# Eight V tiles with copied key windows, one multiply for both table factors, and another order of work

## The chip, the core and the metric

The kernel runs on one core of a Trainium2 chip. A core has TensorE (PE, matrix multiply), VectorE (DVE), ScalarE (ACT), GpSimd (POOL) and SyncE (SP), which only issues transfers here, and 16 DMA engines that all queues share. TensorE reads SBUF and writes PSUM; VectorE and ScalarE take results out of PSUM. The metric is the device time of one execution in microseconds; the profile calls the stretch from the first to the last instruction the span.

## What is computed

Two independent layers on 2048 tokens of 448 features, bfloat16, their outputs side by side in one array of 2048 x 896.

- A is an attention with 16 heads of 28 features. A query at position s sees the keys at s, s-2, ..., s-14, eight of them. `qkv = x @ wqkv`; softmax of the eight scaled scores; weighted sum of the eight V rows; then `@ wo`.
- B is a diagonal state space layer: `h[t] = Lam_bar * h[t-1] + B_bar x[t]` with 448 complex states, and `y = 2 Re(C h) + x * Dskip`.

## The kernel before

**Layout.** Even and odd tokens never meet in A, since the dilation is 2. The kernel views 2048 tokens as 1024 pairs: `xA` holds the transposed input, 7 chunks of 128 features by 1024 pair positions, and every A tile carries both parities. A and B are interleaved in one program.

**A.** Projections contract 448 features per parity on half the rows of the array each: `pair` (lines 521 to 533) issues seven pairs of matmuls (lines 528 and 529), four in a first part and three in a second, with a GpSimd tick between. `V` is projected in nine blocks of 128 pair positions that start every 112 (`k0(b) = 112 * b`), so that each attention block has all its keys, its own and the 14 earlier ones, in one V tile: `Vt[:, par, b]`, with a column of ones behind each head's 28 features for the sum of weights. Blocks overlap in 16 positions, which are computed twice. Q and K are projected in three column ranges (256, 256 and 512 wide; in the text "wide" tiles are the last) by four feature groups. Attention block b then has two score nodes `s0b`, `s1b` (mask matmul L702, score matmuls L706), four exps (L712, `x..`), the weighted sum `a{b}` (32 matmuls, L724), a normalization `n{b}` on VectorE (L730, L731) and a DMA transpose `ot{b}` on SP (L736). Eight `w` tiles multiply by `wo`.

**B.** Four state groups k and two halves hf of time: `b{hf}{k}` (L764) projects the input, `be` evacuates it, VectorE rotates by a cosine/sine table (`ma`, then `ri`), scans (`sc`, L798), rotates back (`mb`, then `ro`) into `h`, and `y`/`z` tiles (L962 to L976) make the output. `ma` and `mb` are the function `mul`: for the three full groups one multiply of a 2 x 512 tile by the cosine row (L777) and one by the sine row (L778); for the small group two of 512 (L780, L781). The tables come from ScalarE: `t2` (L448) and `t4` (L454); only after them does it load the exp table. B's output matrices `C1`, `C2` and the skip product `Gm` (`g0`, `g1`) are built on the way.

**Order.** `Plan` (lines 33 to 113) lists nodes with a cost per engine, what they depend on, which ring of buffers they take from and which they free. It plays them engine by engine on its own clock and always starts the ready node with the lowest rank; `RANK` (line 27) gives each family of nodes an offset and a slope, and nodes that free PSUM go first. A node that can run on ScalarE or VectorE goes to the one that comes free first. The result is a fixed order for each queue. PSUM is a ring "mm" of four two-bank buffers. SP's queue is one list: input transposes, weight loads, then WT transposes, CT transposes, the OT transposes and the stores, each waiting at the head for its own data.

In that order the scores `s00` stand on TensorE behind V, the narrow Q/K tiles and one wide tile (q032); the other seven wide tiles lie between the first attention blocks and B's first projections.

Of the kernel before, what the change touches and what calls it, by code (L numbers as in the profile page):

```python
# [7 lines left out]
BF16 = mybir.dt.bfloat16  # L8
# [8 lines left out]
NB = 9  # L17
# [6 lines left out]
SCALE = float(DH) ** -0.5  # L24


RANK = {"v": (-247.7, 33.131), "q0": (-32.25, 20.848), "q1": (-1351, 261.899), "s": (-328.09, 66.43), "a": (312.95, 100.698), "b0": (348.52, -7.748),
        "b1": (2537.88, -155.645), "d0": (308.87, 213.856), "d1": (1776.4, -98.058), "l": (1991.99, 151.071), "t": (810.76, -33.643), "tk": (305.69, 160.366),
        "xd": (2014.82, -97.299), "cg": (910.27, 8.203), "ch": (1106.04, 1.621), "g": (869.44, 168.173), "y": (701.29, 136.506), "w": (1120.33, 1.167),
        "gu": (1198.03, -204.258), "q2": (787.17, -9.125), "wp": (320.49, 73.04)}  # L30


class Plan:
# [183 lines left out]
def kernel(  # L217
# [40 lines left out]
    tmpB = t_([128, 3584], F32, "tmpB", "rB")  # L258
    Kt = t_([128, 4, 2, NP], BF16, "Kt")
    Qt = t_([128, 4, 2, NP], BF16, "Qt")  # L260
    Vt = t_([128, 2, NB, H, 29], BF16, "Vt")
    Pb = [t_([128, 4, 4, 128], BF16, f"P{i}") for i in range(3)]
    msk = t_([128, 2, 128], BF16, "msk")
    mst = t_([32, 4, 128], BF16, "mst", "rG")
# [39 lines left out]
    SP.dma_start(natW[64:128, 3, D:2 * D], B_B_im[384:448, :])  # L304
    SP.dma_start(Pt[0:64, :], B_B_im[384:448, :])
    SP.dma_start(Pt[64:128, :], B_B_re[384:448, :])
    xbar_x(xB, xB2, 0, 256)
    xbar_x(xB, xB2, 256, 512)


    def sel(o, i, pat, op, fill, base, ch):
# [29 lines left out]
    gms += [lambda e, g=g: G.tensor_copy(msk[32 * g:32 * g + 32, :, :], msk[0:32, :, :]) for g in range(1, 4)]  # L341

    def g_one(e, a):
        G.memset(Vt[:, a, :, :, 28:29].rearrange("p b h o -> p (b h) o"), 1.0)

    def g_zero(e, i):
        if i < 3:
# [190 lines left out]
        behind(k, h["done"][1])  # L538


    plan = Plan({"mm": 4, "P": 3, "O": 3, "wt": 2, "u": 3, "rv": 1, "rs": 1, "ab": 1})
    lazy = {}

    def node(name, cost, fn, deps, rank, **kw):
# [94 lines left out]
    def k0(b):  # L639
        return 112 * b  # L640
# [7 lines left out]
    def at_x(t):  # L648
        return (5.8, 7.3, 9.4, 10.2, 12.0, 12.8, 13.7, 14.6)[(t - 1) // 128]
    vn = {}  # L650
    for b in range(NB):
        h = {}

        def pe(part, b=b, h=h):
            if part == 0:
                h["ps"] = unit()
            pair(h, part, h["ps"], D, lambda o, k: xA[o:o + 64, k, k0(b):k0(b) + 128], lambda o, k: Wv[o:o + 64, k, :])

        def ev(e, b=b, h=h):
            evac(e, Vt[:, :, b, :, 0:28], h["ps"][:, :, 0:D].rearrange("p a (h d) -> p a h d", h=H))  # L660
        n0, n1 = halves(f"v{b}", 0.188, pe, [vw], ("v", b), h, at_x(k0(b) + 128))
        vn[b] = node(f"ev{b}", ab(2 * D), ev, [n1], ("v", b), frees=[(n0, 0)])
    qn = {}
    CH = ((0, 256), (256, 512), (512, 1024))
    for c, (t0_, t1_) in enumerate(CH):
# [21 lines left out]
    for b in range(NB):  # L687
        n = nq(b)
        hb_ = [{}, {}]
        cs = [c for c, (lo, hi) in enumerate(CH) if lo < max(q0(b) + n, k0(b) + 128) and hi > min(q0(b), k0(b))]  # L690
        dep = [qn[q, s, c] for q in range(2) for s in range(4) for c in cs]
        xs = []
        for par in range(2):
            h = hb_[par]
            r = ("s", 2 * b + par)

            def pe(e, par=par, b=b, n=n, h=h):
                c0 = 0 if b == 0 else 16
                u = h["s"] = [unit(), unit()]
                at = lambda g: u[g // 2][:, g % 2]  # L700
                for g in range(4):
                    PE.matmul(at(g)[:, 0:4 * n].rearrange("p (s q) -> p s q", s=4), msk[32 * g:32 * g + 32, 0, :],  # L702
                              msk[32 * g:32 * g + 32, 1:2, c0:c0 + n].to_broadcast((32, 4, n)), start=True, stop=False, skip_group_check=True)
                for s in range(4):
                    for g in range(4):
                        PE.matmul(at(g)[:, s * n:s * n + n], Kt[32 * g:32 * g + DH, s, par, k0(b):k0(b) + 128],  # L706
                                  Qt[32 * g:32 * g + DH, s, par, q0(b):q0(b) + n], start=False, stop=(s == 3), skip_group_check=True)
            i = 2 * b + par

            def ex(e, z, i=i, n=n, h=h):  # L710
                P = h["P"] = Pb[i % 3]
                ACT.activation(P[:].rearrange("p s g q -> p g s q")[:, 2 * z:2 * z + 2, :, 0:n],  # L712
                               h["s"][z][:, :, 0:4 * n].rearrange("p g (s q) -> p g s q", s=4), ACTF.Exp, scale=SCALE)
            n1 = node(f"s{par}{b}", {"P": 0.45}, pe, dep + gm, r, alloc="mm", n=2, mode="q")
            x1 = node(f"x{par}{b}0", {"A": 0.00090 * 8 * n + 0.01}, lambda e, ex=ex: ex(e, 0), [n1, t4], r, alloc="P", frees=[(n1, 0)])
            x2 = node(f"x{par}{b}1", {"A": 0.00090 * 8 * n + 0.01}, lambda e, ex=ex: ex(e, 1), [x1], r, frees=[(n1, 1)])
            xs += [x1, x2]
        h = {}

        def pv(e, b=b, h=h, hb_=hb_):  # L720
            av = h["av"] = unit()
            for par in range(2):
                for hd in range(H):
                    PE.matmul(av[:, par, 29 * hd:29 * hd + 29], hb_[par]["P"][:, hd // 4, hd % 4, :], Vt[:, par, b, hd, :], start=True, stop=True)  # L724

        def nm(e, b=b, n=n, h=h):
            O = h["O"] = wk.tile([128, 2 * D], BF16, tag="O", name="O", bufs=3)
            rc = rcs[0:n, b, :, :]
            avv = h["av"][:, :, 0:29 * H].rearrange("p a (h c) -> p a h c", c=29)
            V.reciprocal(rc, avv[0:n, :, :, 28])  # L730
            V.tensor_tensor(O[0:n, :].rearrange("p (a h d) -> p a h d", a=2, h=H), avv[0:n, :, :, 0:DH],  # L731
                            rc.unsqueeze(3).to_broadcast((n, 2, H, DH)), ALU.mult)
        n3 = node(f"a{b}", {"P": 0.93}, pv, xs + [vn[b]] + g_1 + g_z, ("a", b), alloc="mm", frees=[(xs[0], 0), (xs[2], 0)])
        n4 = node(f"n{b}", {"V": 1.42}, nm, [n3, g_r], ("a", b), alloc="O", frees=[(n3, 0)])
        avs.append(n4)
        ot[b] = node(f"ot{b}", {"S": 1.25}, lambda e, b=b, n=n, h=h: SP.dma_start_transpose(OT()[:, :, q0(b):q0(b) + n], h["O"][0:n, :]),  # L736
                     [n4, t4], b, frees=[(n4, 0)], lat=2.1)
# [16 lines left out]
    for hf in range(2):  # L754
        for k in range(4):
# [13 lines left out]
                evac(e, u[:, 0:n, :], h["ps"][:, 0:n, :])  # L769

            def mul(e, src, k=k, h=h, big=big):
                c, s = tab[:, 0, k, :], tab[:, 1, k, :]
                a = h["a"] = wk.tile([128, 2, HALF], BF16, tag="ra", name="ra", bufs=1)
                x = h[src]
                if big:
                    b = h["b"] = wk.tile([128, 2, HALF], BF16, tag="rb", name="rb", bufs=1)
                    V.tensor_tensor(a[:], x[:], c.unsqueeze(1).to_broadcast((128, 2, HALF)), ALU.mult)  # L777
                    V.tensor_tensor(b[:], x[:], s.unsqueeze(1).to_broadcast((128, 2, HALF)), ALU.mult)  # L778
                else:
                    V.tensor_tensor(a[:, 0], x[:, 0], c, ALU.mult)  # L780
                    V.tensor_tensor(a[:, 1], x[:, 0], s, ALU.mult)  # L781

            def ri(e, k=k, h=h, big=big):
                a = h["a"]
                v = h["v"] = wk.tile([128, 2, HALF], BF16, tag="rv", name="rv", bufs=1)
                if big:
                    b = h["b"]
                    V.tensor_tensor(v[:, 0], a[:, 0], b[:, 1], ALU.add)
                    V.tensor_tensor(v[:, 1], a[:, 1], b[:, 0], ALU.subtract)
                else:  # L790
                    V.tensor_tensor(v[0:64, 0], a[0:64, 0], a[64:128, 1], ALU.add)
                    V.tensor_tensor(v[64:128, 0], a[64:128, 0], a[0:64, 1], ALU.subtract)

            def sc(e, i, k=k, hf=hf, h=h):
                if i == 0:
# [5 lines left out]
            def ro(e, k=k, hf=hf, h=h, big=big):  # L801
                hb, a = hbuf(hf), h["a"]
                to = slice(1, HALF + 1)
                if big:
                    b = h["b"]
                    V.tensor_tensor(hb[:, k, to], a[:, 0], b[:, 1], ALU.subtract)
                    V.tensor_tensor(hb[:, k + 4, to], a[:, 1], b[:, 0], ALU.add)
                    if hf == 0:
                        V.tensor_copy(ini[:, k:k + 5:4], hb[:, k:k + 5:4, HALF])
                else:  # L810
                    V.tensor_tensor(hb[0:64, 3, to], a[0:64, 0], a[64:128, 1], ALU.subtract)
                    V.tensor_tensor(hb[64:128, 3, to], a[64:128, 0], a[0:64, 1], ALU.add)
                    if hf == 0:
                        V.tensor_copy(ini[:, 3:4], hb[:, 3, HALF:HALF + 1])
            rb_, rd_ = (f"b{hf}", k), lambda off, hf=hf, k=k: (f"d{hf}", k, off)
            n1 = node(f"b{hf}{k}", {"P": 3.03 if big else 1.52}, pe, ([wtx[k], wtx[k + 4]] if big else [wtx[k]]) + ([xb1] if hf else []),
                      rb_, alloc="mm", at=24.8)
            n2 = node(f"be{hf}{k}", ab(1024 if big else 512), ev, [n1], rb_, alloc="u", frees=[(n1, 0)])
            m1_ = node(f"ma{hf}{k}", {"V": 1.25 if big else 0.8}, lambda e, mul=mul: mul(e, "u"), [n2, t4], rd_(0), alloc="ab", frees=[(n2, 0)])
            x = ri_ = node(f"ri{hf}{k}", {"V": 0.75 if big else 0.86}, ri, [m1_], rd_(-0.1), alloc="rv", frees=[(m1_, 0)])  # L820
            for i in range(2 if big else 1):
                x = node(f"sc{hf}{k}{i}", {"V": 1.18}, lambda e, i=i, sc=sc: sc(e, i), [x] + ([rout[0, k]] if hf else []), rd_(-0.2),
                         alloc="rs" if i == 0 else None, frees=[(ri_, 0)] if i == (1 if big else 0) else [])
                if i == 0:
                    s0 = x
            m2_ = node(f"mb{hf}{k}", {"V": 1.25 if big else 0.8}, lambda e, mul=mul: mul(e, "s"), [x, t4], rd_(-0.3), alloc="ab", frees=[(s0, 0)])
            free_ = list(wp.values()) if hf == 0 else qdone + vdone + [rout[0, j] for j in range(4)]
            rout[hf, k] = node(f"ro{hf}{k}", {"V": 0.9}, ro, [m2_] + free_, rd_(-0.4), frees=[(m2_, 0)])

# [218 lines left out]
```

## Time and profile before

| What | us |
|---|---|
| median of 14 runs (137.22 to 140.28) | 137.97 |
| profiled execution | 137.74 |
| its span | 136.0 |
| TensorE busy, share of the span | 127.4, 94% |
| VectorE busy | 109.6, 81% |
| ScalarE busy | 89.7, 66% |
| first exp starts | 38.68 |
| last matmul ends | 131.98 |

In the profile, L528 is line 528 of the kernel. A group line gives engine, operation, what it writes and reads, how often, the busy time, the mean ns of one, and the idle time before it with what ended it. A step is the time from one start to the next on an engine; since the end of one instruction overlaps the start of the next, it is shorter than the duration shown. PSUM casts on ScalarE have a step of 0.80 for 896 columns and 0.47 for 512, on VectorE 1.0 and 0.6.

### The profile page before, as it was taken

The numbers are of one execution on the slowest core, as the hardware profiler recorded it, in microseconds if no ns is written. First come the engines' busy times: TensorE is split into PE (matmuls) and PEld (weight loads), VectorE is DVE, ScalarE is ACT, GpSimd is POOL, SyncE is SP. The second block draws the span as 40 slices with busy tenths as digits, with TensorE's granted clock in tenths as the row PEclk, the third lists the DMA queues.
The fourth block names the chain that finished last, engine by engine and source line by source line (L and its number), as shares of the span: only waits on it lengthen the run. The fifth ranks groups of instructions, "written<-read, shape, count | busy, mean of one in ns | idle before, by whom it ended". The sixth has DMA issues, their size and how long they took to land.

```text
span 136.0 us, 3789 instructions
## 1 busy us (share of the span) xinstructions
PE 127.4 (94%) x1530; PEld 70.0 (51%) x1530; DVE 109.6 (81%) x204; ACT 89.7 (66%) x122; POOL 29.0 (21%) x110
## 2 busy tenths in 40 slices
PE   6869989999989999999999999999999999999980
PEld 2225657788434545464544465655665655455540
DVE  0519999999989899999999999999999999911110
ACT  0038999979995966999967998654876227511120
POOL 6985155012799600000000000000000000000000
PEclk9999999999999999999999999999999999999997
DMA  3999999505979578132011008641134778442121
GB/s 92 255 223 308 263 163 195 82 3 99 111 150 192 134 142 165 36 64 59 0 30 34 0 0 64 178 122 67 50 83 109 167 98 277 150 135 72 67 101 43
DMA packets 42754, 15.59 MB, mean 115 GB/s; under 512 B 34926, under 2 KB 42734, under 8 KB 42734
## 3 DMA queue, kind: packets, MB, share of 16 engines
q1 hardware_dynamic: 41264, 14.11, 48.9%
q10 hardware_dynamic: 1374, 1.21, 3.7%
q8 instruction: 13, 0.21, 0.7%
q14 instruction: 7, 0.06, 0.2%
q0 software_dynamic: 96, 0.00, 0.1%
HBM read 3.62 MB, written 3.67 MB: 54 GB/s over the span
## 4 chain that ended last, share of the span: by engine, by line
PE 75%; ACT 15%; DMA 4%; SPq 1%; issue 1%; DVE 0%; ACTq 0%
PE mm L528 23%; PE mm L764 14%; PE mm L962 8%; PE mm L971 8%; PE mm L724 6%; PE mm L964 4%; DMA xA<-in_A_x_dram 4%; PE mm L861 4%; PE mm L702 4%; PE mm L706 3%; ACT Wpad L500 2%; ACT Wpad L501 2%; ACT tab L454 1%; ACT P L712 1%; ACT Wpad L497 1%; ACT tmpB L436 1%
## 5 line engine op out<-in xcount | busy, mean ns | idle before, releaser
L712 ACT ACTIVATE P<-mm 128x896 bf16<-128x896 f32 (+1 forms) x36 | 31.5, 934 | 4.9 <-PE mm L706 4.9
L528 PE MATMUL mm<-xA,Wpad 64*128 64x256 bf16 (+1 forms) x168 | 27.0, 305 | 0.3 <-DVE Qt L507 0.3
L529 PE MATMUL mm<-xA,Wpad 64*128 64x256 bf16 (+1 forms) x168 | 26.8, 305 | 0.1
L505 ACT CAST ys<-mm 128x896 bf16<-128x896 f32 (+2 forms) x15 | 11.3, 770 | 19.1 <-PE mm L971 8.9
L536 POOL MEMSET tick<- 1x1 f32 x41 | 4.9, 119 | 85.4 <-PE mm L529 85.1
L764 PE MATMUL mm<-xB,WT 128*128 128x512 bf16 x98 | 22.5, 379 | 0.3 <-ACT P L712 0.3
L528 PEld LDWEIGHTS <-Wpad 64*128 64x128 bf16 x168 | 15.0, 94 | 7.4 <-POOL tick L536 0.6
L528 PE MATMUL mm<-Wv,xA 64*128 64x448 bf16 x63 | 13.7, 350 | 2.3 <-DMA xA<-in_A_x_dram 1.9
L529 PEld LDWEIGHTS <-Wpad 64*128 64x128 bf16 x168 | 14.8, 94 | 1.6 <-issue 0.8
L764 PEld LDWEIGHTS <-WT 128*128 128x128 bf16 x98 | 9.0, 97 | 11.2 <-issue 1.1
L529 PE MATMUL mm<-Wv,xA 64*128 64x448 bf16 x63 | 13.7, 350 | 0.0
L971 PE MATMUL mm<-C,h 128*128 128x448 bf16 x56 | 11.9, 353 | 0.0
L962 PE MATMUL mm<-C,h 128*128 128x448 bf16 x56 | 11.9, 353 | 0.0
L528 PE MATMUL mm<-wo,OT 64*128 64x448 bf16 x56 | 10.8, 349 | 0.0
L529 PE MATMUL mm<-wo,OT 64*128 64x448 bf16 x56 | 10.8, 349 | 0.0
L731 DVE TENSOR_TENSOR O<-mm,rcs 112x896 bf16<-112x896 f32 (+1 forms) x9 | 9.8, 1091 | 0.3
L507 DVE CAST Vt<-mm 128x896 bf16<-128x896 f32 x6 | 6.4, 1087 | 3.8 <-PE mm L529 3.8
L528 PEld LDWEIGHTS <-xA 64*128 64x128 bf16 x63 | 5.6, 94 | 7.2 <-DMA xA<-in_A_x_dram 2.8
L996 DVE TENSOR_TENSOR ys<-mm,xd 128x448 bf16<-128x448 f32 x3 | 1.9, 624 | 8.5 <-ACT ys L505 8.5
L724 PE MATMUL mm<-Vt,P 128*128 128x29 bf16 x288 | 8.7, 176 | 0.0
L798 DVE TENSOR_TENSOR_SCAN rs<-p_r,ini,rv 128x512 bf16<-128x512 f32 x7 | 8.6, 1269 | 0.0
L798 DVE TENSOR_TENSOR_SCAN rs<-p_r,rv 128x512 bf16<-128x512 f32 x7 | 8.5, 1220 | 0.0
(175 smaller groups left out, 246.3 us busy)
## 6 DMA issues: line engine op xcount, KB each, us to landing
out_dram<-ys SPq DMA_DIRECT2D x15, 224.0 KB, 2.4
Wraw<-in_A_wqkv_dram ACTq DMA_DIRECT2D x2, 336.0 KB, 4.9
wo<-in_A_wo_dram SPq DMA_DIRECT2D x2, 336.0 KB, 3.2
Wv<-in_A_wqkv_dram ACTq DMA_DIRECT2D x1, 336.0 KB, 3.3
natW<-in_B_B_re_dram SPq DMA_DIRECT2D x1, 336.0 KB
natW<-in_B_B_im_dram SPq DMA_DIRECT2D x1, 336.0 KB, 5.1
xo<-in_B_x_dram SPq DMA_DIRECT2D x1, 336.0 KB
out_dram<-ys SPq DMA_DIRECT2D x2, 112.0 KB, 1.7
```

Source lines behind the costliest of these rows:

```text
L505: ACT.copy(o, i)
L507: V.tensor_copy(o, i)
L528: x = PE.matmul(ps[:, a, 0:n], lhs(0, lo[i]), rhs(0, lo[i]), start=(i == 0), stop=(i == 6), skip_group_check=True)
L529: y = PE.matmul(ps[:, b, 0:n], lhs(64, hi[i]), rhs(64, hi[i]), start=(i == 0), stop=(i == 6), skip_group_check=True)
L702: PE.matmul(at(g)[:, 0:4 * n].rearrange("p (s q) -> p s q", s=4), msk[32 * g:32 * g + 32, 0, :], msk[32 * g:32 * g + 32, 1:2, c0:c0 + n].t ...
L712: ACT.activation(P[:].rearrange("p s g q -> p g s q")[:, 2 * z:2 * z + 2, :, 0:n], h["s"][z][:, :, 0:4 * n].rearrange("p g (s q) -> p g s ...
L724: PE.matmul(av[:, par, 29 * hd:29 * hd + 29], hb_[par]["P"][:, hd // 4, hd % 4, :], Vt[:, par, b, hd, :], start=True, stop=True)
L731: V.tensor_tensor(O[0:n, :].rearrange("p (a h d) -> p a h d", a=2, h=H), avv[0:n, :, :, 0:DH], rc.unsqueeze(3).to_broadcast((n, 2, H, DH)) ...
L764: PE.matmul(ps[:, i, :], WT[:, j, 128 * m:128 * m + 128], xB[:, j, HALF * hf:HALF * hf + HALF], start=(j == 0), stop=(j == 6))
L798: V.tensor_tensor_scan(h["s"][:, i], p["r2"][:, k:k + 1].to_broadcast((128, HALF)), h["v"][:, i], 0.0 if hf == 0 else ini[:, m:m + 1], ALU ...
L962: PE.matmul(ps[:, 0, 0:D], hb[:, m, lo:lo + 128], lazy["C2"][:, m, :], start=(m == 0), stop=False, skip_group_check=True)
L971: PE.matmul(ps[:, 1, 0:D], hb[:, m, lo + 1:lo + 129], lazy["C1"][:, m, :], start=(m == 0), stop=(t in YD and m == 6), skip_group_check=True)
```

## The change

1. V is projected in eight aligned blocks of 128 (`Va[:, b]`). Attention blocks 0 and 8 read `Va[:, 0]` and `Va[:, 7]` directly. For each block 1 to 7 a new node `vi{b}` on SP copies a window `vw` by two DMAs in SBUF: the last 16b partitions of `Va[:, b-1]` and the first 128 - 16b of `Va[:, b]`. `vw` has one buffer: `vi{b}` needs `a{b-1}` to have run, and `a{b}` needs `vi{b}`.
2. `mul` writes one tile `a[128, 2, 2, 512]`, both factors by both input rows, in one multiply (2048 elements, or 1024 for the small group); `rb` is gone.
3. The first half of `xB` is transposed in four pieces of 128 columns, not two of 256.
4. `RANK` has other numbers and a family "vi". The order that results, as built:
   - TensorE ahead of the first scores: V 0 to 5, then narrow Q/K tiles with V 6 and V 7 between, then the wide tiles q102 and q002 (second part of q002 behind s00). After that: `b00 s10 b01 s01 a0 b03 s11 b02 s02 a1`, wide q112, q012, `s12`, wide q122, q022, `s03`, wide q132, q032, `a2 s13 b13 s04 b12 a3 s14 b11 s05 a4 b10 s15 g0 s06 g1 s16 a5 y0 z0 s07 y1 z1 s17 a6 y2 s08 z2 a7 s18 y3 a8 z3`, then the w tiles and y4 to z7 as before.
   - before: `b00 s10 b01 s01 a0 b03 s11 b02 s02 a1`, wide q132, q022, `s12`, wide q122, q012, `s03 a2`, wide q112, q002, `s13`, first part of q102, `b13`, its second part, `a3 b12 s04 b11 s14 b10 s05 a4 g0 s15 g1 s06 a5 y0 s16 z0 y1 s07 z1 a6 s17 y2 s08 z2 a7 s18 y3 z3 a8`.
   - Up to the first exp, ScalarE no longer pads the weight tile wp00 (VectorE does), evacuates V 1, 4, 5, 6, 7 (before: 1, 6, 8), seven narrow Q/K tiles (before: eight) and the wide q102. VectorE evacuates V 0, 2, 3 (before: 0, 2, 3, 4, 5, 7).
   - Later, eq022 and be10 are on VectorE; be13, ge0 and we1 on ScalarE; xd4 and xd6 stand ahead of the last rotation on VectorE.
   - SP: `vi1` between the xB pieces and the Ctn loads; then `ot0`, the CT transposes, `vi2 ot1 vi3 ot2 vi4 ot3 vi5 ot4`, the four wo loads, `vi6 ot5 yo0 yo1 vi7 ot6 yo2`, the xo loads, `ot7 ot8 yo3` and the stores.

```diff
-    xbar_x(xB, xB2, 0, 256)
-    xbar_x(xB, xB2, 256, 512)
+    for i in range(4):
+        xbar_x(xB, xB2, 128 * i, 128 * i + 128)
...
-    for b in range(NB):
+    for b in range(8):
...
-            pair(h, part, h["ps"], D, lambda o, k: xA[o:o + 64, k, k0(b):k0(b) + 128], lambda o, k: Wv[o:o + 64, k, :])
+            pair(h, part, h["ps"], D, lambda o, k: xA[o:o + 64, k, 128 * b:128 * b + 128], lambda o, k: Wv[o:o + 64, k, :])
...
+    for b in range(1, NB - 1):
+        h = {}
+
+        def win(e, b=b, h=h):
+            h["w"] = wk.tile([128, 2, H, 29], BF16, tag="vw", name="vw", bufs=1)
+            SP.dma_start(h["w"][0:16 * b], Va[128 - 16 * b:128, b - 1])
+            SP.dma_start(h["w"][16 * b:128], Va[0:128 - 16 * b, b])
+        vw_[b] = h, node(f"vi{b}", {"S": 1.1}, win, [vn[b - 1], vn[b]] + g_1, ("vi", b), alloc="vw", lat=2.1)
+
+    def window(b):
+        return Va[:, 0] if b == 0 else Va[:, 7] if b == NB - 1 else vw_[b][0]["w"]
...
-                    PE.matmul(av[:, par, 29 * hd:29 * hd + 29], hb_[par]["P"][:, hd // 4, hd % 4, :], Vt[:, par, b, hd, :], start=True, stop=True)
+                    PE.matmul(av[:, par, 29 * hd:29 * hd + 29], hb_[par]["P"][:, hd // 4, hd % 4, :], v[:, par, hd, :], start=True, stop=True)
...
-        n3 = node(f"a{b}", {"P": 0.93}, pv, xs + [vn[b]] + g_1 + g_z, ("a", b), alloc="mm", frees=[(xs[0], 0), (xs[2], 0)])
+        n3 = node(f"a{b}", {"P": 0.93}, pv, xs + [vw_[b][1]] + g_1 + g_z, ("a", b), alloc="mm",
+                  frees=[(xs[0], 0), (xs[2], 0)] + ([(vw_[b][1], 0)] if 0 < b < NB - 1 else []))
...
-                    V.tensor_tensor(a[:], x[:], c.unsqueeze(1).to_broadcast((128, 2, HALF)), ALU.mult)
-                    V.tensor_tensor(b[:], x[:], s.unsqueeze(1).to_broadcast((128, 2, HALF)), ALU.mult)
+                    V.tensor_tensor(a[:], x[:].unsqueeze(1).to_broadcast((128, 2, 2, HALF)), tab[:, :, k, :].unsqueeze(2).to_broadcast((128, 2, 2, HALF)), ALU.mult)
                 else:
-                    V.tensor_tensor(a[:, 0], x[:, 0], c, ALU.mult)
-                    V.tensor_tensor(a[:, 1], x[:, 0], s, ALU.mult)
+                    V.tensor_tensor(a[:, 0], x[:, 0:1].to_broadcast((128, 2, HALF)), tab[:, :, k, :], ALU.mult)
...
-                    V.tensor_tensor(v[:, 0], a[:, 0], b[:, 1], ALU.add)
-                    V.tensor_tensor(v[:, 1], a[:, 1], b[:, 0], ALU.subtract)
+                    V.tensor_tensor(v[:, 0], a[:, 0, 0], a[:, 1, 1], ALU.add)
+                    V.tensor_tensor(v[:, 1], a[:, 0, 1], a[:, 1, 0], ALU.subtract)
```

## The prediction

> **What bounds the kernel now.** I read the share of busy time first, then the same by stage, then the chain that ended last, then the costliest groups and the DMA issues. The busy line of the page:
>
> ```profile
> PE 127.4 (94%) x1530; PEld 70.0 (51%) x1530; DVE 109.6 (81%) x204; ACT 89.7 (66%) x122; POOL 29.0 (21%) x110
> ```
>
> The stages, cut where the chain changes its engine (columns: stretch, its length, then busy us and instructions of each engine, clock, DMA share, GB/s):
>
> ```profile
> 8.27:26.67 18.40, 17.54 (x227) 11.25 (x227) 16.22 (x47) 17.13 (x31) 7.63 (x33) 1.00 1.01 212
> 26.67:40.67 14.00, 13.45 (x186) 8.60 (x186) 13.08 (x21) 13.18 (x17) 7.36 (x32) 1.00 0.56 93
> 40.67:67.01 26.34, 26.34 (x356) 13.07 (x356) 25.34 (x44) 21.88 (x27) 6.48 (x20) 1.00 0.50 103
> 67.01:107.19 40.18, 40.18 (x556) 22.65 (x554) 39.09 (x68) 29.60 (x39) 0.00 (x0) 1.00 0.34 72
> 107.19:131.98 24.79, 24.79 (x192) 12.69 (x189) 13.30 (x23) 7.64 (x12) 0.70 (x8) 1.00 0.46 127
> ```
>
> From 40.67 to 131.98 TensorE is never idle at full clock. Before 40.67 it has holes, and ScalarE and VectorE are about as full. The chain in order of time (start, us, what) shows the seam:
>
> ```profile
> 35.36 2.01 ACT tab L454
> 37.39 1.28 ACT L712
> 38.68 1.95 ACT P L712 x2
> 40.67 3.18 PE mm L764 x14
> ...
> 51.81 0.32 PE mm L528
> ...
> 54.94 0.30 PE mm L702 x4
> ...
> 130.37 1.32 PE mm L971 x7
> ```
>
> ScalarE finishes the second table (t4), loads its exp table and makes the first P; only then does TensorE get PSUM for b01 at 40.67, and it sets the time to the end. So I add up two numbers: when ScalarE reaches the first exp, and how much TensorE work lies behind b01.
>
> A rule that speaks against this reading: the Trainium skill, "Perfetto Trace Analysis", section "Identifying the Most-Contended Engine", calls matmul busy time a poor measure of TensorE and wants the weight-load share. That is 51% here; by it VectorE at 81% would be the bound, and a removed matmul worth nothing. But in the chain the starts of 448-column pairs lie 0.19 us apart and of 512-column pairs 0.21, back to back, with VectorE waiting for PE. By the rule the TensorE term below is 0, by the row 1.7. I take the row.
>
> **Term 1, TensorE behind b01.** The V tile v8 (7 pairs at 0.19 = 1.33 us) lay ahead of b01, at 26.67 to 28.93. Its room is not left empty: ahead of the first scores the new order has 2 wide Q/K tiles (tokens 512 to 1024: q102, q002), where the old one had 1 (q032). So behind b01 there are 6 wide tiles instead of 7. The old seven in the trace: two from 51.81 to 54.94 (3.13), two 55.44 to 58.65 (3.21), two 60.06 to 63.22 (3.16), and the last in two pieces around b13, 0.99 + 0.76 = 1.75. The new six are three such pairs, unsplit: 9.50 against 11.25, -1.75. Two a blocks and one s block no longer border on a wide tile (0.82 against 0.90, 0.50 against 0.52), about -0.15. In return b13 now follows s13 at once and needs the PSUM that eq032 empties: ScalarE has cg10, cg11 and eq132 before it, 0.1 to 0.2 late. Sum -1.75 - 0.15 + 0.15 = -1.75; I take -1.7. All other matmuls behind b01 are the same, in another order.
>
> **Term 2, ScalarE up to the first exp.** Between the first V evacuation (10.61) and the first exp (38.68) ScalarE loses one Wpad tile (wp00, 2.95, the step from one such tile to the next work) and one 512-wide evacuation (0.47), and gets one 1024-wide (0.91) and two V evacuations (0.80 each): -0.91. VectorE takes wp00 (2.0) and one 512-wide evacuation (0.6), and loses three V evacuations (1.0 each): -0.4. But ScalarE had only 0.8 us of waiting there, and gets more: its new evacuations follow their matmuls at once. TensorE reaches the end of q131, by adding its tiles from 8.27 (V 1.33, 256-wide Q/K 0.77, and 0.6 at q001 for wp00 on VectorE), at about 28.8; ScalarE is there at 28.2. Then it waits 0.3 each for q020 and q130, and 0.15 for q102. From q131 on: 3 x 0.47 + 0.6 of waits, t2 1.81, two wtmp 1.14, wide evacuation 0.91 + 0.15, t4 and table load 3.3. That puts the first exp at about 38.4: -0.3. Bounds: -0.9 if no wait is added, +0.6 if wp00 or the evacuations run twice that late.
>
> **Term 3, the window copies.** Seven blocks (1 to 7) now read a copy made by two DMAs on SP. The parts overlap: issue 0.5 to 0.6 us each. Nothing in the trace copies SBUF to SBUF in plain form, so I bound the landing by neighbours (issues: x count, KB, median us to landing):
>
> ```profile
> out_dram<-ys SPq DMA_DIRECT2D x15, 224.0 KB, 2.4
> natW<-in_B_B_im_dram SPq DMA_DIRECT2D x1, 336.0 KB, 5.1
> OT<-O SPq DMA_TRANSPOSE x9, 2.8
> CT<-Ctn SPq DMA_TRANSPOSE x4, 2.4
> ```
>
> A window is 128 rows of 1856 B, 238 KB. Nearest is the 224 KB store: 2.4. The second part starts 0.6 after the first, so 3.0 from the first issue; the far end is the load in the crowded early stage, 5.1 + 0.6 = 5.7. The stretches where windows are copied move 36 to 110 GB/s (GB/s row), so I take 3.0, up to 3.6 where an output store is in flight.
>
> One buffer: window b is issued when a(b-1) has run and must land before a(b). The room, in new TensorE order: window 3 has s13 b13 s04 b12 = 0.5 + 1.6 + 0.5 + 3.1 = 5.7; window 4 has s14 b11 s05 = 4.1; 5 has b10, g0, g1 and three s, 10.5; 6 has 8.2; 7 has y2 s08 z2 = 2.1 + 0.5 + 1.5 = 4.1. Less 0.2 for the end of a(b-1), 3.9 stands against 3.0: hidden, by 0.9. Window 2 waits instead for SP, which is in the CT transposes until 57.25 as now: landed near 60.3, and a2, moved behind the third pair of wide tiles, comes at about 62. Window 1 has 25 us.
>
> A rule against this: the Trainium skill, "DMA: Bandwidth & Descriptors", section "Rules for kernel authors", advises against two transfers to disjoint partition ranges, since they serialize on the same 16 engines, and for one transfer of 128. If the second part began only when the first had landed, a window would take 2 x 2.4 = 4.8, be 0.9 late at a4 and at a7, and the total would be -2.0 + 1.8 = -0.2. The row: two stores issued at 111.24 and 112.01 land at 114.26 and 114.97, each 3.0 after its issue. They overlap, so I keep 3.0 for two.
>
> What stands behind the waiting windows on SP: behind window b the transpose ot(b-1), which needs a(b-1) anyway; behind window 1 the Ctn loads and WT transposes. xB in four pieces costs 4 x 1.34 (step of the 128-column xA pieces) against 4.21, +1.15; window 1 adds 1.1. Ctn ends at 24.95 instead of 22.68, WT's first transpose goes 0.4 later than 24.54; it landed at 27.72 and is read at 36. The next six wait for natW on VectorE, not for SP. Window 6 stands behind the four wo loads, which wait for the last C2 tile near 85 and take 2.2 to issue: out near 87.5, landed near 90.5, due at a6 near 94. Window 7 stands behind y1's store, issued about when a6 ends. Cost 0, and what is lost with the cover is each us over 3.9, at a4 and at a7.
>
> **Term 4, the multiply.** Two multiplies of 1024 elements become one of 2048 (twelve times), two of 512 one of 1024 (four times):
>
> ```profile
> L777 DVE TENSOR_TENSOR ra<-u,tab 128x1024 bf16<-128x1024 bf16 x6 | 4.1, 689 | 0.2
> L781 DVE TENSOR_TENSOR ra<-u,tab 128x512 bf16<-128x512 bf16 x2 | 0.8, 419 | 0.0
> ```
>
> 512 more elements cost 0.27, so 2048 take 0.689 + 0.534 = 1.22, a step of 1.2 to the next; the pair's step is 1.33 (54.71 to 56.04). Saved 12 x 0.13 + 4 x 0.14 = 2.1 us of VectorE. Behind b01 VectorE also gets eq022 and be10 (1.14 each) and a scaling (0.48), and gives be13 (0.6), ge0 and we1 (1.0 each) to ScalarE: +0.15. It is 95 to 97% busy from 40.67 to 107.19 but not on the chain: the last rotation ends at 116.13, y4 needs it at 117.89. VectorE becomes 2.0 shorter, TensorE's y4 comes 2.0 earlier, two xd multiplies (1.1) now stand ahead of that rotation instead of we1 (1.0): room still about 1.7. So the multiply is worth 0 itself, and keeps VectorE from being the next bound. Below a gain of nothing it could only lose: at 1.5 per product it would be 12 x 0.3 = 3.6 longer, 1.9 over its room, and all of the gain gone.
>
> **Sum.** -1.7 - 0.3 + 0 + 0 = -2.0. Behind the last matmul nothing changes (131.98 to 136.0). The profiled execution, 137.74 with a span of 136.0, goes to 135.7 and a span of 134.0. The median shown is 137.97, 0.2 above it; taking the same 2.0 off gives 136.0. A difference under 0.3% (0.4 us) is about what a measurement of this kernel cannot tell from none.
>
> **Rivals.**
> *Windows late, slower.* Place: a4 and a7, price: the excess over 3.9, twice; from 5.6 also a2 and a3. The change breaks even at 4.9 from first issue to landing; at 5.7, as the crowded load, it is 2 x 1.8 + 1.5 - 2.0 = +3.1, 141.1. For: 5.1 rows exist, y1's store is in flight at window 7. Against: every copy issued after 60 in the trace that has a landing time lands within 4.3 of its issue. A mild form, 4.4, gives -1.0: 137.0.
> *VectorE bounds, slower.* If the four-dimensional product loses the [...]rate that its rows have, 2048 elements take about 2.3 (estimated from the PSUM casts, which run without that rate: 512 in 0.684, 1024 in 1.225); 12 x 1.1 + 4 x 0.5 = +15 on an engine with 1.7 us of room: about 149. Against: the same operands with a repeated factor run at that rate now.
> *The early stage gains nothing or loses.* Holes ahead of q001 and q131 push the first exp to +0.6: -1.7 + 0.6 = -1.1, 136.9.
> *Room was never used.* If the wide tile placed early is paid for by a later first exp in full (1.5), what is left is -0.5: 137.5.
>
> **How the numbers follow.** Forecast 0.68, with its own range 135.3 to 136.6. Early stage worse 0.09 (faster), mild lateness 0.08 (faster 0.06, same 0.02), room not used 0.05 (same 0.04, faster 0.01), windows late 0.07 and VectorE 0.03 (slower). Faster 0.68 + 0.09 + 0.06 + 0.01 = 0.84, of which I move 0.03 to slower for order effects that the sums don't see: 0.81. Same 0.06, slower 0.13. The range 135.2 to 137.7 leaves out the slower cases and the tail of a larger gain (term 2 at -0.9).
>
> **What would show it.** Right: first exp near 38.4; only six wide Q/K tiles behind b01; span of TensorE without holes from b01 to the end; the windows' second part landing about 3 us after the first issue; products of 1.2 us; y4 near 116. Wrong: PE weight loads of the a blocks waiting for DMA vw at a4 or a7; products over 1.35; TensorE waiting for h or Gm at y0 or y4; ScalarE waiting over 2 us ahead of its t4.

## The result, and the profile after

| What | before | after |
|---|---|---|
| median, us | 137.93 of 47 runs (137.16 to 140.28) | 135.86 of 10 runs (135.34 to 138.47) |
| profiled span, us | 136.0 | 133.6 |
| first exp starts | 38.68 | 37.75 |
| b01 starts | 40.67 | 39.74 |
| last matmul ends | 131.98 | 129.52 |

The ratio is 0.986, with a 95% interval of 0.9837 to 0.9883: faster by 2.1 us. The prediction was 136.0.

The busy line of the page after:

```profile
PE 126.5 (95%) x1516; PEld 70.3 (53%) x1516; DVE 107.5 (80%) x191; ACT 88.2 (66%) x118; POOL 28.2 (21%) x109
```

The stages after, cut at the same pieces of work as far as the new order has them (stretch, its length, busy us and instructions of PE, PEld, DVE, ACT and POOL, clock, DMA share, GB/s):

```profile
7.76:26.16 18.40, 18.11 (x250) 12.74 (x250) 16.27 (x52) 16.93 (x30) 8.11 (x35) 1.00 1.02 207
26.16:39.74 13.58, 12.74 (x170) 7.52 (x166) 12.64 (x20) 12.67 (x16) 6.91 (x31) 1.00 0.71 123
39.74:68.14 28.40, 28.16 (x376) 14.22 (x376) 27.06 (x41) 23.59 (x29) 6.04 (x18) 1.00 0.53 110
68.14:104.69 36.55, 36.55 (x521) 21.13 (x520) 35.72 (x55) 25.55 (x33) 0.00 (x0) 1.00 0.45 105
104.69:129.52 24.83, 24.83 (x191) 12.61 (x189) 13.24 (x22) 9.14 (x13) 0.87 (x8) 1.00 0.41 128
```

From b01 to the end of the last matmul it is 89.78 us, where it was 91.31 (to its start, which I use below, 89.62 and 91.15). TensorE has one hole there, 0.24 us in the third row. The seam in the chain in order of time (start, us, what), and the one place behind it that leaves TensorE:

```profile
34.43 2.00 ACT tab L454
36.45 1.28 ACT L724
37.75 1.95 ACT P L724 x2
39.74 3.18 PE mm L778 x14
...
59.12 0.91 ACT P L724
60.03 1.11 ACT wtmp L511 x2
61.14 0.90 ACT Kt L505
62.04 0.92 ACT Qt L505
63.01 1.67 PE mm L778 x7
```

The seam is the same three steps, 0.93 earlier. At 63.01 b13 waits until ScalarE has emptied the PSUM of q032: this is the hole of 0.24.

The products on VectorE, 12 of 2048 elements (busy, mean ns of one, idle before):

```profile
L789 DVE TENSOR_TENSOR ra<-rs,tab 128x2048 bf16<-128x2048 bf16 x6 | 7.3, 1223 | 0.2
L789 DVE TENSOR_TENSOR ra<-u,tab 128x2048 bf16<-128x2048 bf16 x6 | 7.3, 1223 | 0.1
```

And one window on SP's queue, the fourth (start, us to issue):

```profile
69.13 0.51 SPq L669 DMA_DIRECT2D vw<-Va  x1
69.74 0.54 SPq L670 DMA_DIRECT2D vw<-Va  x1
70.86 1.44 SPq L750 DMA_TRANSPOSE OT<-O  x1
```

By the trace its parts landed at 72.49 and 72.77, 3.64 from the first issue, and a4 started at 73.16. No attention block waits for a window in this trace.

**Where the time came from.** The first V matmuls wait for xA's transfer in every profile, and that transfer's arrival varies: here v1 starts at 7.76, before at 8.27. So I measure the first exp from the start of V 1's evacuation (10.10 here, 10.61 before). From there it is 27.65 us after and 28.07 before: the order gains 0.42, and the other 0.51 of the earlier first exp is this execution's transfer. From b01 on the gain is 1.53. Together 1.95 by the profile; the medians say 2.07. Two parts of the edit were not tried by themselves: xB in four pieces and the evacuations that change engine.

### The profile page after: what moved, and what is told of

Same layout as the page of the kernel before. It is cut to its first block, busy times and chain, and to the rows that moved or that the text cites. A ratio compares the mean times of both kernels' runs of the same rounds, so it can differ in the third digit from the quotient of the medians.

```text
span 133.6 us, 3771 instructions
## 1 busy us (share of the span) xinstructions
PE 126.5 (95%) x1516; PEld 70.3 (53%) x1516; DVE 107.5 (80%) x191; ACT 88.2 (66%) x118; POOL 28.2 (21%) x109
## 4 chain that ended last, share of the span: by engine, by line
PE 79%; ACT 10%; DMA 4%; DVE 2%; issue 2%; ACTq 0%
PE mm L528 26%; PE mm L778 14%; PE mm L970 8%; PE mm L979 8%; PE mm L737 5%; PE mm L972 5%; DMA xA<-in_A_x_dram 4%; PE mm L869 4%; PE mm L714 3%; PE mm L718 2%; ACT P L724 2%; ACT wtmp L511 2%; PE mm L529 2%; ACT Kt L505 2%; ACT tab L454 2%
## 5 line engine op out<-in xcount | busy, mean ns | idle before, releaser
L505 ACT CAST ys<-mm 128x896 bf16<-128x896 f32 (+2 forms) x16 | 12.2, 779 | 22.3 <-PE mm L979 8.9
L529 PE MATMUL mm<-xA,Wpad 64*128 64x256 bf16 (+1 forms) x168 | 26.5, 305 | 0.0
L528 PE MATMUL mm<-xA,Wpad 64*128 64x256 bf16 (+1 forms) x168 | 26.4, 305 | 0.1
L528 PEld LDWEIGHTS <-Wpad 64*128 64x128 bf16 x168 | 15.3, 94 | 6.9
L529 PEld LDWEIGHTS <-Wpad 64*128 64x128 bf16 x168 | 15.0, 94 | 0.9 <-issue 0.5
L528 PE MATMUL mm<-Wv,xA 64*128 64x448 bf16 x56 | 12.4, 356 | 0.5 <-DMA xA<-in_A_x_dram 0.3
L529 PE MATMUL mm<-Wv,xA 64*128 64x448 bf16 x56 | 12.3, 355 | 0.0
L737 PEld LDWEIGHTS <-P 128*128 128x128 bf16 x288 | 8.1, 96 | 1.3 <-issue 0.4
L505 ACT CAST u<-mm 128x1024 bf16<-128x1024 f32 (+1 forms) x6 | 5.2, 870 | 4.7 <-PE mm L778 4.5
```

Source lines behind the costliest of these rows:

```text
L505: ACT.copy(o, i)
L528: x = PE.matmul(ps[:, a, 0:n], lhs(0, lo[i]), rhs(0, lo[i]), start=(i == 0), stop=(i == 6), skip_group_check=True)
L529: y = PE.matmul(ps[:, b, 0:n], lhs(64, hi[i]), rhs(64, hi[i]), start=(i == 0), stop=(i == 6), skip_group_check=True)
```

## The experiments

**The changed kernel once more**, to see how it repeats.

> The changed kernel itself, as the yardstick on this chip. Theory and rivals alike: 135.9 us, 2.0 under the kernel before.

Measured: 135.84, ratio 0.9873 (0.9832 to 0.9913). From V 1's evacuation up to a3 TensorE's work starts at the same times, within 0.02. At a4 it is another case (engine, what it waited for, us, times, longest; then SP's queue):

```profile
PE mm L737 <- DMA vw<-Va: 0.2, 1, 0.2
```

```profile
69.13 0.51 SPq L669 DMA_DIRECT2D vw<-Va  x1
69.74 1.78 SPq L670 DMA_DIRECT2D vw<-Va  x1
```

The second copy took 1.78 us to issue instead of 0.54 and landed at 73.33, 4.2 from the first issue, and a4 waited 0.2. So the cover at a4 is as thin as 0.4 in one execution and gone in the next. In five more traces below with the same windows (the doubled blocks, the pairs and the moved selects) window 4 took 3.4 to 3.8, and a4 did not wait.

**Two multiplies per product in the changed kernel**, all else the same; the small group likewise.

```diff
-V.tensor_tensor(a[:], x[:].unsqueeze(1)..., tab[:, :, k, :].unsqueeze(2)..., ALU.mult)
+for i in range(2):
+    V.tensor_tensor(a[:, i], x[:], tab[:, i, k, :].unsqueeze(1)..., ALU.mult)
```

> The changed kernel with each product made by two multiplies again, all orders kept. Theory (TensorE bounds behind b01, the multiply is worth nothing itself): VectorE gets 2.1 us longer, of which the room ahead of y4 takes most; by the 1.7 us of room in the prediction +0.3, by the 0.8 us between ro10 and y4 in the changed kernel's trace up to +1.2, so 136.2 to 137.1. Rival (VectorE bounds, the single multiply is the gain): the whole 2.1, 138.0.

Measured: 136.41, ratio 0.9901 (0.9866 to 0.9936), against 135.84 in the same set of runs. In the trace, from b01 to the last matmul, it is 89.78, against 89.62 and 89.86 in the two of the changed kernel; the 0.24 more of the second is a4's late window, which this run does not have. So the trace says +0.16, the medians +0.6 with intervals that overlap: the size is loose, but small. The trace shows that VectorE is at the edge. VectorE's last rotation, and who waited for it at y4 (waits from 112 to 118 us):

```profile
113.98 1.29 DVE L790 TENSOR_TENSOR ra<-rs,tab 128x1024 bf16<-128x1024 bf16 x2
115.31 0.43 DVE L816 TENSOR_TENSOR h<-ra 128x512 bf16<-128x512 bf16 x1
115.65 0.42 DVE L817 TENSOR_TENSOR h<-ra 128x512 bf16<-128x512 bf16 x1
```

```profile
PEld L972 <- DVE h L817: 0.4, 1, 0.4
```

The rotation ends at 116.07 and y4 starts at 116.12. In the changed kernel it ends at 114.60, 0.84 before y4. So the pair takes just the room that the single multiply had left, and the 0.16 is lost there.

The same run corrects the size of the saving. Summed over the 16 products, the steps to the next VectorE instruction, without waits, are 18.43 with pairs and 17.32 with single multiplies: 1.1, not 2.1. One product of the changed kernel and what follows it:

```profile
53.64 1.22 DVE L789 TENSOR_TENSOR ra<-rs,tab 128x2048 bf16<-128x2048 bf16 x1
54.90 0.43 DVE L814 TENSOR_TENSOR h<-ra 128x512 bf16<-128x512 bf16 x1
```

The step is 1.26, a little longer than the product's 1.22 and not shorter, and the pair's was 1.33.

**The single multiply alone in the kernel before**, the small group likewise.

```diff
-V.tensor_tensor(a[:], x[:], c..., ALU.mult)
-V.tensor_tensor(b[:], x[:], s..., ALU.mult)
+V.tensor_tensor(a[:], x[:].unsqueeze(1)..., tab[:, :, k, :].unsqueeze(2)..., ALU.mult)
```

> The kernel before with the single multiply alone, all orders kept. Theory (VectorE is not on the chain, 1.8 us of room ahead of y4): no change, 137.9, within 0.3. Rival (VectorE bounds): up to -2.1, 135.8.

Measured: 137.31 against 137.36, ratio 0.9995 (0.9968 to 1.0023). From b01 to the last matmul it is 91.14 against 91.15 in the trace, with 1.1 us less of VectorE (steps 17.65 against 18.78). A shorter VectorE is worth nothing there.

**TensorE work behind b01**: b12's first seven matmuls are done twice, with the same result.

```diff
-for j in range(7):
+for j in list(range(7)) * (2 if i == 0 and (hf, k) == (1, 2) else 1):
```

> The same doubling in b12, behind b01. Theory (TensorE bounds behind b01): +1.5, 137.4. Rival (VectorE or ScalarE bounds there): 0 to +0.5, 135.9 to 136.4.

Measured: 137.67, ratio 0.9997 (0.9961 to 1.0034), +1.8 on the changed kernel by medians and +1.47 in the trace from b01 to the last matmul, for 1.5 us of matmuls. Work behind b01 counts one for one.

**The same matmuls ahead of the first exp**: b00's seven twice, `(hf, k) == (0, 0)`.

> The changed kernel in which b00, ahead of the first exp, does its first seven 512-column matmuls twice (1.5 us more of TensorE, same result). Theory (ScalarE sets the first exp, TensorE has 1.35 us of waiting at s10 and 0.3 at b01): +0.0 to +0.2, 135.9 to 136.1. Rival (every TensorE microsecond counts): +1.5, 137.4.

Measured: 137.54, ratio 0.9982 (0.9956 to 1.0009): +1.7. My theory, 0 to 0.2, was wrong, and the rival that TensorE's work counts everywhere seemed right. But the first exp did not move: 27.63 us behind V 1's evacuation. The loss sits later, on TensorE's second block. The waits from 36 to 53 us:

```profile
DVE u L507 <- PE mm L778: 1.7, 1, 1.7
...
PE mm L778 <- DVE O L744: 1.3, 1, 1.3
```

b02 waits for PSUM that the first normalization frees, and that stands on VectorE behind the first product. VectorE's rows there (start, us), and GpSimd's of the same time:

```profile
39.61 1.23 DVE L507 CAST u<-mm 128x1024 bf16<-128x1024 f32 x1 [1.73 <-PE mm L778]
40.94 2.50 DVE L789 TENSOR_TENSOR ra<-u,tab 128x2048 bf16<-128x2048 bf16 x1
...
46.40 0.33 DVE L743 RECIPROCAL rcs<-mm 128x32 f32<-128x32 f32 x1
```

```profile
40.32 1.04 POOL L312 TENSOR_SCALAR_AFFINE_SELECT dgO<-dsr 128x128 bf16<-128x128 bf16 x4
41.32 1.03 POOL L312 TENSOR_SCALAR_AFFINE_SELECT dgE<-dsr 128x128 bf16<-128x128 bf16 x4
```

The product took 2.50 instead of 1.24. Its start had been pushed into GpSimd's eight selects. In the changed kernel the same two engines meet the other way: the product starts first, runs in 1.24, and the small GpSimd operation beside it takes 1.12, until the product ends, where its like takes 0.18:

```profile
39.33 1.24 DVE L789 TENSOR_TENSOR ra<-u,tab 128x2048 bf16<-128x2048 bf16 x1
38.58 0.18 POOL L466 TENSOR_TENSOR p_sg<-p_gr,p_sgn 128x1 f32<-128x1 f32 x1
39.50 1.12 POOL L466 TENSOR_TENSOR p_sh<-p_hr,p_sgn 128x1 f32<-128x1 f32 x1
```

The Trainium skill, "SBUF — State Buffer", section "Who interferes with whom", says that a VectorE instruction with two inputs in SBUF, as this product has, contends with a GpSimd instruction that reads SBUF, and that the order of issue decides which of them blocks; these rows agree. But that was still only a reading, so the next two runs separate the matmuls from the selects.

**b00's seven twice, with the selects moved 16 GpSimd operations earlier.** In the written-out order dgO0 to dgE3 stand before the eleventh operation of the chain of small GpSimd operations instead of behind its last.

```diff
-... p3b9 p3b10 ... p3b25 dgO0 dgO1 dgO2 dgO3 dgE0 dgE1 dgE2 dgE3
+... p3b9 dgO0 dgO1 dgO2 dgO3 dgE0 dgE1 dgE2 dgE3 p3b10 ... p3b25
```

> The changed kernel with b00's first seven matmuls done twice (the result is the same), as in the run before, and with GpSimd's eight selects (dgO, dgE) moved ahead of the last 16 small GpSimd operations, so that they run near 36.8 us and not beside the first product on VectorE (ma00). Theory: the doubled matmuls themselves cost little, and the 1.7 us came from ma00 at 2.5 us instead of 1.24; with the selects away ma00 is back near 1.25, n0 starts near 45.2 instead of 46.4, and the time is 136.1 to 136.4. Rival: TensorE work ahead of the first exp counts one for one, the selects are a coincidence: 137.4 to 137.7 again.

**The control: that move alone.**

> The changed kernel with only the eight selects moved earlier, to tell what the move does by itself. Theory: nothing that can be measured, 135.6 to 136.1, since ma00 took 1.24 us in the changed kernel. Rival: the small GpSimd operations that now run beside ma00, or the C tiles that wait for them, make it 0.4 to 1.0 slower.

Measured in the same set of runs: 136.38, ratio 0.9883 (0.9849 to 0.9918), with the doubled matmuls, and 136.41, ratio 0.9879 (0.985 to 0.9908), without. The doubled matmuls now cost nothing that shows. In the trace the product is back:

```profile
40.40 1.22 DVE L541 CAST u<-mm 128x1024 bf16<-128x1024 f32 x1 [1.74 <-PE mm L812]
41.73 1.23 DVE L823 TENSOR_TENSOR ra<-u,tab 128x2048 bf16<-128x2048 bf16 x1
```

Measured from V 1's evacuation, the last matmul starts 0.28 later than in the control (119.54 against 119.26), where the first form lost 1.56. So 1.3 of the 1.6 us came from the selects; the rival, TensorE one for one ahead of the exp, falls. The control's median is 0.5 above the changed kernel's but in another set of runs; its ratio is inside the repeat's interval, and its trace takes the same 119.26 us as the changed kernel's.

**Nine V tiles in the changed kernel's order**, no windows; the ninth tile's second part goes between V 7's two parts.

```diff
-for b in range(8):          # aligned blocks, 128 * b
+for b in range(NB):         # k0(b), as before
...
-            av, v = unit(), window(b)
+            av = unit()
```

> The changed kernel's order and multiply, but V in nine overlapping tiles without window copies; the ninth tile (1.33 us of TensorE, 0.8 of ScalarE) stands between narrow Q/K tiles, ahead of q102. Theory (the ninth tile's room is what the second wide tile uses): q102 and so t4 come later by 1.3 less the 0.6 to 1.2 that ScalarE waits ahead of it, plus 0.8 of evacuation on ScalarE: +0.8 to +1.3, 136.7 to 137.2. Rival A (the order alone is the gain): +0.0 to +0.3, 135.9 to 136.2. Rival B (the copies cost something): under 135.9.

Measured: 138.31, ratio 1.0045 (1.0018 to 1.0071): 2.5 more than the changed kernel, slower than either theory gave. Its profiled execution had its V tiles 2.6 us late (a wait of 1.5 for xA, then half clock), so I ran it again, beside a form with the selects moved.

> Nine V tiles in the changed kernel's order, no window copies, as run before (138.31), once more for a profile whose first V tiles aren't late. Theory: 138.0 to 138.4 again; the ninth tile's matmuls (1.33) and its evacuation on ScalarE (0.8) push the first exp by 1.0 to 1.5, and the rest is a first product of 2.5 us beside GpSimd's selects. Rival: ma00 is at 1.25 and the first exp itself is 2.0 or more later than 37.75, so that all of the loss is on ScalarE.

> Nine V tiles as in the run beside it, with the eight selects moved earlier. Theory: if ma00 and the selects meet there, 136.8 to 137.3, about 1.2 less than with nine tiles alone. Rival: no difference, 138.0 to 138.4, and the ninth tile costs all of it ahead of the first exp.

Measured: 139.04 of four runs, ratio 1.0126 (1.0067 to 1.0184), and 138.45, ratio 1.0055 (1.0022 to 1.0088) with the selects moved. The rivals of both runs were right. The first product takes 1.25 and 1.23, and the first exp is 29.87 us behind V 1's evacuation instead of 27.65: +2.2, all ahead of the exp. ScalarE's rows of the nine-tile kernel, run again, show it:

```profile
25.52 0.67 ACT L545 ACTIVATE wtmp<-natW,p_nb 128x448 f32<-128x448 bf16 x1
27.70 0.91 ACT L539 CAST Vt<-mm 128x896 bf16<-128x896 f32 x1 [1.51 <-PE mm L563]
28.50 0.59 ACT L539 CAST Qt<-mm 128x512 bf16<-128x512 f32 x1
```

ScalarE waits 1.51 for the ninth tile and takes 0.8 to evacuate it. Part of this is the place that I gave it, so 2.2 is not the price of a ninth tile in general; it shows that a ninth tile does not fit into this order for its 0.8 of ScalarE alone. The run has a second reading, and it is the better one: from b01 to the last matmul it takes 89.63, the changed kernel with its seven windows 89.62. The windows cost nothing there.

**The windows in the old order**: eight V tiles and the copies in the kernel before, all other nodes as they stood, vi2 behind the CT transposes.

```diff
-... ctn0                     ... ot1 ...
+... vi1 ctn0                 ... vi2 ot1 vi3 ot2 ...
```

> The kernel before in its own order, the ninth V tile left out, V in eight tiles with window copies. Theory: the first exp comes 0.5 to 0.9 earlier (ScalarE loses one evacuation, TensorE 1.33 us of which part was waited for), behind b01 nothing is saved; window 2 leaves SP behind the CT transposes near 57.3, lands near 60.3 and is 1.2 late for a2 at 59.1; so +0.3 to -0.6 in all, 137.3 to 138.2. Rival (the tile itself is the gain): -1.3, 136.6.

Measured: 141.05, ratio 1.0181 (1.0116 to 1.0247): slower, where I had expected a small gain or little. The first exp came only 0.37 earlier behind V 1's evacuation, where 0.5 to 0.9 was expected. a2 stands earlier in that order, and window 2 comes out of SP at 56.96 and lands at 60.44 (waits from 58 to 61 us):

```profile
PE mm L771 <- DMA vw<-Va: 2.3, 1, 2.3
```

That is 2.3, but from b01 to the last matmul the trace lost 4.0. The rest is in the granted clock, the third figure from the end (same columns as the stages above):

```profile
58.00:60.50 2.50, 0.28 (x20) 0.12 (x12) 1.27 (x2) 2.50 (x4) 0.00 (x0) 1.00 0.76 164
60.50:61.88 1.38, 1.30 (x36) 1.10 (x38) 0.31 (x1) 1.34 (x3) 0.00 (x0) 1.00 0.10 20
61.88:65.29 3.41, 3.41 (x18) 1.24 (x16) 3.34 (x5) 0.00 (x0) 0.18 (x2) 0.50 1.13 112
65.29:67.00 1.71, 1.71 (x32) 0.76 (x30) 1.50 (x5) 1.25 (x2) 0.00 (x0) 1.00 0.10 18
```

A stall of 2.3 us was followed by 3.4 us at half clock. From a2 to s13 the same matmuls take 5.70 instead of 4.05, +1.65, and 2.29 + 1.65 = 3.94 is the loss.

The slow clock does not follow every time. 3.4 us at half clock in a span of 139.3 make a mean of 0.988, which is this trace's. Four of the kernel's six executions have that mean and took 140.99 to 142.05; two have 1.00 and took 139.39, 2.0 above the kernel before and 1.6 under the fastest of the four. 137.36 less the 0.37 ahead of the first exp and with the stall of 2.29 is 139.28, so by their times TensorE stalled in those two as well and the clock stayed. Of the kernel before, one of 23 executions in the same set has 0.988, and six and three of 23 in the two other sets: the slow clock also comes without this stall, but less often.

**Windows made late in the changed kernel**: the first part of each is copied twice, the second time onto the same rows.

```diff
 SP.dma_start(h["w"][0:16 * b], Va[128 - 16 * b:128, b - 1])
+SP.dma_start(h["w"][0:16 * b], Va[128 - 16 * b:128, b - 1])
```

> The changed kernel with the first part of each window copied twice (the same data; the second copy waits for the first to land), so that a window lands about 5.4 us after its first issue instead of 3.0 to 3.6. Theory (room 3.9 us at windows 4 and 7, 5.5 at window 3): 1.5 late at a4 and at a7, 0 to 0.3 at a3, +2.5 to +3.5, 138.4 to 139.4. Rival (room is wider, the chain takes it up later): under +1.

Measured: 143.22, ratio 1.0334 (1.0268 to 1.0399), +7.4 by medians of two sets of runs against +2.5 to 3.5 expected. The repeated copy waits for the first to land (window 4's rows):

```profile
70.48 0.52 SPq L669 DMA_DIRECT2D vw<-Va  x1
73.74 0.49 SPq L670 DMA_DIRECT2D vw<-Va  x1
74.28 0.59 SPq L671 DMA_DIRECT2D vw<-Va  x1
```

So windows 2 to 7 land 5.4 to 6.4 after their first issue. TensorE waits 0.8 at a2, 0.5 at a3, 2.2 at a4 (put down there to ScalarE's exp, but the weight load ahead of it waits for DMA vw) and 1.9 at a7: 5.4. Behind a4 the clock falls again:

```profile
74.00:76.70 2.70, 0.58 (x21) 0.32 (x20) 2.05 (x5) 2.58 (x4) 0.00 (x0) 1.00 0.57 121
76.70:78.37 1.67, 1.55 (x35) 1.21 (x37) 0.56 (x2) 1.17 (x3) 0.00 (x0) 1.00 0.33 66
78.37:81.78 3.41, 3.41 (x10) 1.22 (x8) 3.27 (x5) 1.26 (x2) 0.00 (x0) 0.50 0.24 78
81.78:84.00 2.22, 2.22 (x29) 1.02 (x28) 1.50 (x2) 1.00 (x2) 0.00 (x0) 1.00 0.67 148
```

From a4 to g0 it takes 6.12 instead of 4.44: +1.7. 5.4 + 1.7 = 7.1, of 7.2 lost in the trace from b01 to the last matmul. Behind a7's wait of 1.9, and behind the 1.3 of b02 in the doubled b00, the clock stays at 1.00.

## Why the prediction was right, point by point

- **What bounds the kernel.** Right. 1.5 us of matmuls behind b01 cost 1.5 in the trace (b12 doubled); 1.1 us less of VectorE gained nothing in the old kernel. By the weight-load share (51%, now 53%) neither would have followed.
- **Term 1, TensorE behind b01: -1.7 predicted, -1.53 measured.** The wide tiles, from start to start, take 9.44 where the old seven took 11.15: -1.71, against -1.75 predicted. b13 waits 0.24 where 0.15 was put. What is left, 0.06 where 0.15 was put, would be the blocks that no longer border on a wide tile; it is a difference, not a measured size.
- **Term 2, first exp: -0.3 predicted, -0.42 measured** from V 1's evacuation on. Counted from where v1 started before, the first exp stands at 38.26; the 37.75 of this trace has 0.51 of luck in xA's transfer. The way was right: ScalarE waited 0.52 ahead of q131 and 0.18 each ahead of q020 and q130, where 0.6, 0.3 and 0.3 were put. But the sum was not: the parts listed from q131 on make 9.3 and the first exp 28.8 + 9.3 = 38.1, not 38.4, so by its own parts Term 2 was -0.6 and the forecast -2.3. That the total of -2.0 meets the measured 1.95 so closely is luck: Term 1 came out 0.2 short, and Term 2 beyond the -0.3 that was written.
- **Term 3, the windows: 0 predicted, 0 shown** (89.62 with, 89.63 without). The second part landed 2.9 to 3.0 from the first issue at windows 3, 5 and 7, as taken from the two stores; so the copies overlap, and the rule from the Trainium skill, "DMA: Bandwidth & Descriptors", section "Rules for kernel authors", read as one landing after the other, would have put them at 4.8. Window 4 took 3.6 and once 4.2: the bound "up to 3.6" was too low, and the cover at a4 was thinner than said. At window 6 the first part alone took 4.6 and landed at 91.97, 1.8 ahead of a6; the GB/s row of the page before shows 122 to 178 there, not the 36 to 110 that the prediction read off for all windows. The break-even of 4.9 was too kind as well: the price of a late window is not always the lateness alone, since a stall of 2.2 was followed by half clock that cost 1.7 more. That the old order lost 3.9 with the same copies shows what moving a2 behind the third pair of wide tiles does: in the changed kernel a2 starts at 61.29, and window 2's second part, issued at 56.46, is there without a wait.
- **One size in Term 3 was far off and cost nothing.** WT's first transpose went from 24.54 to 27.73, not 0.4 later: window 1, in the crowded early stage, took 5.7 to land, and the Ctn loads behind it were issued late too. The second WT transpose still landed at 33.81, ahead of b00 at 34.76: the cover was there, but 0.95 wide.
- **Term 4, the multiply: the duration was right, the saving twice too large.** 1.22 predicted and measured; but I took the step to the next instruction as 1.2, and it is 1.26, so the 16 products save 1.1 instead of 2.1. That it is worth nothing by itself is shown in the old kernel. The missing 1.0 is about what the room ahead of y4 is short of: 0.84 instead of 1.7. So VectorE is the next bound, as I wrote, but at half the distance.
- **The rivals.** "VectorE bounds" fell with the 1.22. "The early stage loses" fell with the first exp. "Room was never used" fell in the undisturbed doubling of b00: 1.5 us of matmuls ahead of the exp cost 0.28. "Windows late" did not happen but is near, and dearer than I priced it.

What was right for a poor reason: I wrote that TensorE's room ahead of the first exp was free, with ScalarE as the only other limit. VectorE's way from b00 to the first normalization had 0.76 of room, and which of VectorE and GpSimd starts first decides whether that is enough.

## What to carry to other kernels

Find the instruction from which the bound engine is never idle, and price an edit by the side it falls on: work moved ahead of it was nearly free here, work left behind it cost its full time. Price a transfer's cover with its spread, not its median, and a stall of 2 us on TensorE with the slow clock that may follow it, which nearly doubled the loss here in four executions of six. When an edit shifts a VectorE operation, look at what GpSimd does in that moment before blaming the edit.

## What the runs showed of the hardware that was not expected

- **The clock after a stall.** In two traces waits of 2.2 and 2.3 us were followed, 1.3 to 1.6 us after TensorE had begun again, by a granted clock of 0.50 for 3.41 us, and 1.65 to 1.7 us were lost on top; after waits of 1.3 and 1.9 it stayed at 1.00. The length of the wait alone does not decide: two of six executions of the kernel with the wait of 2.3 kept the full clock by their means and times, and in the profile of the nine tiles that came late a wait of 1.5 near the start was followed by the same 3.41 us (rows below). The Trainium skill, "TensorE: Matmul & The Clock Gate", section "HAM oscillation — how this bites in real kernels", speaks of idle gaps above about 3.4 us; here less was enough. What else decides, these runs don't tell.

```profile
7.20:9.00 1.80, 0.30 (x4) 0.11 (x4) 0.00 (x0) 0.00 (x0) 1.54 (x7) 1.00 1.26 160
9.02:12.43 3.41, 3.41 (x22) 1.28 (x20) 0.97 (x1) 1.28 (x1) 1.95 (x7) 0.50 1.19 305
```

- **GpSimd and VectorE.** A product of two bf16 inputs took 2.50 instead of 1.24 behind a run of GpSimd selects that had started 0.6 earlier, and 1.23 with the selects moved away; the other way round a run of four selects took 2.83 instead of 1.04 beside VectorE's work.
- **Issue time.** Window 4's second copy took 0.54 us to issue in one execution of the changed kernel and 1.78 in the next, and 1.36 and 1.29 in the two runs with b00 doubled, with the same copies ahead of it in SP's order; the cause was not looked for.
